# Transposed tokens copied by ScalarE, three experts' weights moved behind the first gathers, last attention pair normalised in two parts

## The chip, the cores and the metric

The kernel runs on one core of one Trainium2 chip. The metric is the device time of one execution in microseconds (us); lower is better. TensorE (PE) multiplies matrices, VectorE (DVE) and ScalarE (ACT) read its results from PSUM, GpSimd (POOL) issues most of the DMAs, SyncE (SP) issues the rest. Each engine works through its own instructions in order and waits on semaphores for the others.

## The reference

Two layers. The first is a block-causal attention over 8 batches, 8 heads, 576 positions and head size 64: scores in blocks of 64, softmax, times v. Its result, with heads side by side, is a matrix x of 4608 tokens by 512. The second is a mixture of experts with a given expert per token:

```python
x = attn_out.transpose(0, 2, 1, 3).reshape(B * S, H * D)      # 4608 x 512
for e in range(E):                                            # 8 experts
    mask = domain_id == e
    h = np.maximum(x[mask] @ w1[e], 0.0)                      # 512 -> 1024
    out[mask] = h @ w2[e]                                     # 1024 -> 512
```

## The kernel before

**Attention.** The 8 batches have 4 head pairs each, so there are 32 pairs p, and the loop at L469 emits pair p's scores (`emit_G`, L354) beside pair p-1's product with v (`emit_P` L408, `emit_Q` L413). For one pair PE transposes q and k of a later pair into PSUM tiles `PT` (L335), DVE copies them to `QK` (L339), PE makes scores into `ps` (L347, L373), ACT takes the exponential (L352), and PE multiplies by v into `po` (L398, L403), with a column of ones giving the row sums. At the end of `emit_Q` DVE takes a reciprocal (L419) and multiplies (L420) into the tile `x` of the batch, in half precision. `po` has two PSUM banks: blocks 1 to 3 of the pair in bank 0, blocks 4 and 0 in bank 1. `store_x` (L433) writes finished rows to the DRAM buffer `x_rows`, by SP; the last pair's 128 columns go out by one DMA of SP (64 rows) and one of ACT (512 rows).

**Weights.** `loads` (L450) runs on POOL's queue. From pair 20 on, it emits the weights of experts 0 to 3, two pieces per pair. An expert has 8 pieces (`w1_piece` L119, `w2_piece` L122), each read as 512 KB of single precision and written as 256 KB of half precision. 26 of the 32 pieces are emitted inside the pair loop; the other 6, of expert 3, at L609. POOL does not wait for the pairs there. A DMA on POOL's queue waits until the DMA issued eight places earlier has landed, since eight semaphores go round.

**Bridge.** After the last pair, PE runs 36 matmuls whose result is not used (L515). POOL gathers rows of `x_rows` by token index into `xg` (`gather`, L524; five indirect DMAs of 128 rows for an expert), and has to wait for every store of `x_rows`.

**Experts.** Each expert has 640 slots in five blocks of 128 tokens. `transpose_block` (L534) turns a gathered block on PE into a PSUM tile `pt` (L537, two buffers) and copies it to `xT` (L540, DVE). `mm1` (L553) makes eight groups of 8 matmuls (L559) into `ph` (two buffers), each followed by ACT's rectifier into `hT` (L565). `mm2` (L570) makes five blocks of 8 matmuls (L576) into `po` (two buffers); DVE copies each to `osb` (L582, ten buffers) and POOL scatters the rows to the output (L583). The transposes of expert e+1 stand between the blocks of `mm2` of expert e. For expert 0, `mm1` is run in two halves (L617): three blocks transposed, half 0, two more blocks, half 1. The gathers of expert e+2 stand ahead of `mm1` of expert e, and the weights of expert e+3 between the scatters of `mm2` of expert e, for e of 1 and more (L628).

A last loop (L636) handles experts with more than 640 tokens; its count is read from the data.

Of the kernel before, what the change touches and what calls it, by code (L numbers as in the profile page):

```python
# [9 lines left out]
F32 = mybir.dt.float32  # L10
# [3 lines left out]
ALU = mybir.AluOpType  # L14
# [4 lines left out]
def kernel(  # L19
# [10 lines left out]
    nc = tc.nc  # L30
    B, H, S, D = q.shape
    N = B * S
    E = moe_w1.shape[0]
    DM = moe_w1.shape[1]
# [2 lines left out]
    CAP = 128 * NB  # L37
    NJ = N // 128
    HP = H // 2
    NQ = NJ // 4  # L40

    ctx.enter_context(tc.manual_schedule())
    xd = nc.dram_tensor("x_rows", (N, DM), F16, kind="Internal").ap()
# [6 lines left out]
    asb = att.enter_context(tc.tile_pool(name="asb", bufs=1))  # L50
    aps = att.enter_context(
        tc.tile_pool(name="aps", bufs=1, space=bass.MemoryType.PSUM))
# [22 lines left out]
    def load_v(eng, b, ns):  # L75
# [11 lines left out]
        out=dom_i[:],  # L87
        in_=moe_domain_id.bitcast(I32).rearrange("(p c) -> p c", p=128))
    load_qk(0, 0, 1)
    for c in range(5):  # L90
        n = min(128, S - 128 * c)
        nc.sync.dma_start(
            out=vst[0][0:n, c],
            in_=v[0, :, 128 * c : 128 * c + n, :].rearrange("h p d -> p h d"))
# [4 lines left out]
    identh = const.tile([128, 128], F16, name="identh")  # L99
# [49 lines left out]
    def load_expert(e):  # L149
        if e % 4 == 3:  # L150
            w1s[e], w2s[e], t = load_vst(moe_w1[e], moe_w2[e])
        else:
            w1s[e], w2s[e], t = load_weights(wsb, 3, moe_w1[e], moe_w2[e])
        return t
# [12 lines left out]
    for i in range(2):  # L167
        n = 5 * HP * 66
        nc.scalar.copy(
            out=VE[i][:].rearrange("p m g z -> p (m g z)").bitcast(F32),  # L170
            in_=z_f[:].to_broadcast([128, n]))
        nc.scalar.copy(out=ATE[i][:, 64:832].bitcast(F32),
                       in_=z_f[:].to_broadcast([128, 384]))
# [4 lines left out]
    po = aps.tile([128, 2, 512], F32, name="po")  # L178
# [229 lines left out]
    def emit_P(st):  # L408
        for m in range(1, 4):
            emit_pv(st, m - 1, m)  # L410


    def emit_Q(st):  # L413
        hp = st["p"] % HP
        emit_pv(st, 3, 4)
        emit_pv(st, 4, 0)
        rc = asb.tile([128, 2, 3, 2], F32, name="rc", tag="rc", bufs=2)
        pv = po[:, :, 0:396].rearrange("p b (w z) -> p b w z", z=132)
        nc.vector.reciprocal(out=rc[:], in_=pv[:, :, :, 1:131:129])  # L419
        nc.vector.tensor_tensor(  # L420
            out=st["x"][:, :, 128 * hp : 128 * hp + 128].rearrange(
                "p (b w) (i z) -> p b w i z", b=2, i=2),
            in0=pv[:, :, :, 2:130].rearrange("p b w (i z) -> p b w i z", i=2),
            in1=rc[:].unsqueeze(4).to_broadcast([128, 2, 3, 2, 64]), op=ALU.mult)

    def emit_VE(b):
        for i in range(2):
# [2 lines left out]
                out=VE[b % 2][64 * i : 64 * i + 64, :, :, cs],  # L430
                in_=vS[b % 3][0:64, :, :, cs])

    def store_x(b, c0, c1, eng):  # L433
        x = xs[b]
        nc.sync.dma_start(out=xd[S * b : S * b + 64, c0:c1], in_=x[64:128, 4, c0:c1])
        eng.dma_start(
            out=xd[S * b + 64 : S * b + S, c0:c1].rearrange("(m p) d -> p m d", p=128),
            in_=x[:, 0:4, c0:c1])

    npair = B * HP  # L440
    rout, tabl = routing(), table()
    next(rout)
    QKs = {0: emit_T(0)}
# [3 lines left out]
    w1s, w2s, wts = {}, {}, []  # L447


    def loads(p):  # L450
        fn = nc.gpsimd.tensor_copy
        for b in range(2, B):
            if p == max(0, 4 * b - 10):
                load_qk(b)
                load_v(nc.gpsimd, b, range(0, 5))
                cast_v(fn, b - 1)
                load_v(nc.gpsimd, b, range(5, H + 1))
        if p == 4 * B - 12:
            cast_v(fn, B - 1)
            for e in range(4):  # L460
                wts.extend(load_expert(e))
        if p >= 4 * B - 12:
            for f in wts[:2]:
                f()
            del wts[:2]

    xs = []
    prev = None
    for p in range(npair + 1):  # L469
        b, hp = divmod(p, HP)  # L470
        st = None
        if p < npair:
            st = {"p": p, "QK": QKs.pop(p)}
            if hp == 0:
                x_t = asb.tile([128, 6, DM], F16, name="x", tag="x", bufs=4)
                xs.append(x_t)
            st["x"] = x_t
            emit_G(0, st)
        if p:
            if p + 2 < npair:  # L480
                QKs[p + 2] = emit_T(p + 2)
        if p < npair:
            emit_G(1, st)
        if prev is not None:
            emit_P(prev)
        if p < npair:
            emit_G(2, st)
        if prev is not None:
            emit_Q(prev)
            if prev["p"] == npair - 2:  # L490
                store_x(B - 1, 0, DM - 128, nc.sync)
            elif prev["p"] == npair - 1:
                store_x(B - 1, DM - 128, DM, nc.scalar)
            elif prev["p"] % HP == HP - 1:
                done = prev["p"] // HP
                for xb in {2: (0,), 3: (1,), 4: (2,), 5: (3, 4, 5), 6: (6,)}.get(done, ()):
                    store_x(xb, 0, DM, nc.sync)
        if p == 0:
            cast_v(nc.scalar.copy, 0)
            QKs[1] = emit_T(1)  # L500
            emit_VE(0)
            QKs[2] = emit_T(2)
        if p < npair and hp == 3 and b + 1 < B:
            emit_VE(b + 1)
        for _ in range(2 if p % 4 else 1):
            if p > 1:
                next(tabl, None)
        loads(p)
        prev = st
    for _ in tabl:  # L510
        pass

    ps = aps.tile([128, 2, 512], F32, name="ps", tag="ps", bufs=2)
    for i in range(36):
        nc.tensor.matmul(out=ps[:, i % 2], lhsT=identh[:], rhs=w1s[0][:, 0, 0:512],  # L515
                         start=True, stop=True)
    att.close()


# [1 line left out]
    mps = ctx.enter_context(  # L521
        tc.tile_pool(name="mps", bufs=1, space=bass.MemoryType.PSUM))

    def gather(tok):  # L524
        g = msb.tile([128, NB, DM], F16, name="xg", tag="xg", bufs=3)
        for blk in range(NB):
            nc.gpsimd.indirect_dma_start(  # L527
                out=g[:, blk, :], out_offset=None, in_=xd,
                in_offset=bass.IndirectOffsetOnAxis(
                    ap=tok[:, 1, blk : blk + 1], axis=0),  # L530
                bounds_check=N - 1, oob_is_err=False)
        return g

    def transpose_block(g, xT, blk):  # L534
        pt = mps.tile([128, 4, 128], F16, name="pt", tag="pt", bufs=2)
        for dc in range(4):
            nc.tensor.transpose(  # L537
                out=pt[:, dc], in_=g[:, blk, 128 * dc : 128 * dc + 128],
                identity=identh[:])
        nc.vector.tensor_copy(out=xT[:, :, 128 * blk : 128 * blk + 128], in_=pt[:])  # L540


    def w1_cols(w1h, dc, fc):
# [6 lines left out]
    def new_hT():  # L550
        return msb.tile([128, 8, CAP], F16, name="hT", tag="hT", bufs=2)

    def mm1(xT, hT, w1h, halves=(0, 1)):  # L553
        hw = CAP // 2
        for fc in range(8):
            ph = mps.tile([128, 2, 512], F32, name="ph", tag="ph", bufs=2)
            for dc in range(4):
                for i in halves:
                    nc.tensor.matmul(  # L559
                        out=ph[:, i, 0:hw],  # L560
                        lhsT=w1_cols(w1h, dc, fc),
                        rhs=xT[:, dc, hw * i : hw * i + hw],
                        start=(dc == 0), stop=(dc == 3))
            i0, i1 = halves[0], halves[-1] + 1
            nc.scalar.activation(  # L565
                out=hT[:, fc].rearrange("p (i n) -> p i n", i=2)[:, i0:i1],
                in_=ph[:, i0:i1, 0:hw], func=AF.Relu)
# [23 lines left out]
    def tok_of(e):  # L591
        return tok0[:, :, NB * e : NB * e + NB]
# [12 lines left out]
                                op0=ALU.arith_shift_right)  # L605
        nc.vector.memset(base_f[:], float(NB * E))

    xgs = {e: gather(tok_of(e)) for e in range(2)}
    for f in wts:  # L609
        f()  # L610
    xT = new_xT()
    for e in range(E):
        if e + 2 < E:
            xgs[e + 2] = gather(tok_of(e + 2))
        hT = new_hT()
        if e == 0:
            for i, blks in enumerate(((0, 1, 2), (3, 4))):  # L617
                for blk in blks:
                    transpose_block(xgs[0], xT, blk)
                mm1(xT, hT, w1s[0], (i,))  # L620
        else:
            mm1(xT, hT, w1s[e])
        nxt = None
        if e + 1 < E:
            xT = new_xT()
            nxt = (xgs[e + 1], xT)
        todo = ()
        if e and e + 3 < E:  # L628
            todo = load_expert(e + 3)
        if e == 1:  # L630
            count_rounds()
        mm2(hT, w2s[e], tok_of(e), outs[NB * e : NB * e + NB], todo, nxt)
# [50 lines left out]
```

## Time and profile before

The median of five runs is 335.2 us (333.94 to 336.11). The profiled execution took 334.62 us, of which the profile's span covers 333.0 us.

| what | value |
|---|---|
| profiled execution, whole | 334.62 us |
| its span | 333.0 us |
| PE busy | 273.8 us, 82% of the span |
| DVE busy | 160.3 us, 48% |
| ACT busy | 146.1 us, 44% |
| POOL busy | 205.4 us, 62% |
| mean granted clock of PE | 0.945 |
| last product with v, start | 145.39 us |
| first gather, start | 152.19 us |
| first matmul of `mm1`, expert 0 | 158.84 us |
| first matmul of `mm2`, expert 0 | 172.42 us |
| last matmul block ends about | 319.5 us |

Times are from the start of the span. In the tables a line names its source line (L559), the engine, the operation, output and inputs by the names in the program, and the idle time of the engine just before it with what ended that idle time. PEld is PE's loading of stationary operands, which runs beside its matmuls. The end of a matmul in the trace is a model, its start is measured. The granted clock is the share of full speed at which PE was allowed to run.

### The profile page before, as it was taken

To read this page: it belongs to the slowest core of one execution; us is meant where nothing else is said; L and a number is where in the kernel's file an instruction comes from. 1 tells how busy PE (TensorE), PEld (TensorE's weight loads), DVE (VectorE), ACT (ScalarE), POOL (GpSimd) and SP (SyncE) were. 2 spreads that over 40 slices of the span, in tenths; PEclk is the share of its full clock that TensorE was granted. 3 is DMA by queue.
4 is the path that set the end of the run, shared out by engine and by line. 5 is a ranking of instruction groups with operands and counts; after the bars stand their busy time and mean duration, and the time that the engine had idled before them with its cause. 6 is when DMAs were issued, how large, how long until landed. Compare 5 with 4: busy or idle time off the path is not lost. (4 is left out here: it accounts for less than half of the span.)

```text
span 333.0 us, 8592 instructions
## 1 busy us (share of the span) xinstructions
PE 273.8 (82%) x3658; PEld 176.9 (53%) x3658; DVE 160.3 (48%) x298; ACT 146.1 (44%) x208; POOL 205.4 (62%) x274
## 2 busy tenths in 40 slices
PE   2588787947899987885899789989898998999930
PEld 1366555635577765552555455647465564656510
DVE  3869899979789787621015123050422404042120
ACT  5658556827499877820350331505033150513200
POOL 8669999899883643205884718767785875223230
PEclk9999789959699999999699999999999999999995
DMA  8999999999991999992395309959798894112030
GB/s 162 201 214 209 176 260 193 243 207 189 240 267 28 205 212 231 216 245 64 106 178 184 113 18 194 263 118 237 189 214 213 153 237 150 74 46 96 32 114 0
DMA packets 36472, 55.68 MB, mean 167 GB/s; under 512 B 9838, under 2 KB 22638, under 8 KB 36432
## 3 DMA queue, kind: packets, MB, share of 16 engines
q0 software_dynamic: 26128, 49.17, 68.3%
q1 hardware_dynamic: 9776, 5.81, 6.5%
q8 instruction: 30, 0.49, 0.6%
q10 hardware_dynamic: 528, 0.13, 0.2%
q14 instruction: 10, 0.08, 0.1%
HBM read 67.15 MB, written 15.20 MB: 247 GB/s over the span
## 5 line engine op out<-in xcount | busy, mean ns | idle before, releaser
L352 ACT ACTIVATE A<-ps 128x1024 f16<-128x1024 f32 (+1 forms) x96 | 83.1, 883 | 42.3 <-PE ps L347 30.1
L565 ACT ACTIVATE hT<-ph 128x640 f16<-128x640 f32 (+1 forms) x72 | 46.1, 644 | 121.6 <-PE ph L559 97.8
L583 POOL DMA_INDIRECT out_dram<-osb,tok x40 | 40.5, 1012 | 55.4 <-DVE osb L582 43.5
L540 DVE COPY xT<-pt 128x512 f16<-128x512 f16 x40 | 16.9, 424 | 111.2 <-PE pt L537 85.7
L559 PE MATMUL ph<-xT,w1h 128*128 128x320 f16 x384 | 56.8, 307 | 5.2 <-issue 2.5
L576 PE MATMUL po<-w2h,hT 128*128 128x512 f16 x240 | 56.7, 379 | 3.2 <-DVE osb L582 2.7
L527 POOL DMA_INDIRECT xg<-x_rows,tok x40 | 40.5, 1012 | 26.1 <-DMA x_rows<-x 14.2
L559 PEld LDWEIGHTS <-w1h 128*128 128x128 f16 x384 | 38.4, 100 | 23.4 <-issue 6.2
L78 POOL DMA_DIRECT2D vst<-in_v_dram x56 | 42.5, 786 | 10.1 <-DMA kh<-in_k_dram 4.3
L576 PEld LDWEIGHTS <-hT 128*128 128x128 f16 x320 | 30.1, 98 | 34.4 <-issue 4.9
L339 DVE COPY QK<-PT 128x576 f16<-128x576 f16 x64 | 45.6, 749 | 3.2 <-PE PT L335 2.9
L347 PE MATMUL ps<-QK 64*128 64x512 f16 (+3 forms) x256 | 37.0, 328 | 2.7 <-ACT A L352 1.1
L403 PE MATMUL po<-vS,A 128*128 128x65 f16 x640 | 36.5, 201 | 1.3 <-issue 1.3
L398 PE MATMUL po<-VE,ATE 128*128 128x130 f16 x160 | 32.9, 232 | 4.6 <-DVE x L420 3.5
L582 DVE COPY osb<-po 128x512 f32<-128x512 f32 x40 | 27.4, 684 | 18.8 <-PE po L576 18.8
L403 PEld LDWEIGHTS <-A 128*128 128x128 f16 x640 | 32.0, 102 | 4.0 <-issue 4.0
L420 DVE TENSOR_TENSOR x<-po,rc 128x768 f16<-128x768 f32 x32 | 30.6, 957 | 1.1
L335 PE MATMUL PT<-identh,kh 64*64 64x64 f16 x576 | 17.0, 204 | 10.8 <-DVE inv L234 6.0
L114 POOL CAST vS<-vst 128x1024 f16<-128x1024 f32 (+1 forms) x21 | 19.1, 962 | 5.9 <-DVE QK L339 5.9
L335 PEld LDWEIGHTS <-kh 64*64 64x64 f16 x576 | 14.8, 119 | 12.3 <-issue 9.6
L398 PEld LDWEIGHTS <-ATE 128*128 128x128 f16 x160 | 16.0, 100 | 9.5 <-issue 7.3
L335 PE MATMUL PT<-identh,qh 64*64 64x64 f16 x576 | 16.7, 203 | 4.1 <-DVE QK L339 3.4
(88 smaller groups left out, 274.9 us busy)
## 6 DMA issues: line engine op xcount, KB each, us to landing
vst<-in_v_dram POOLq DMA_DIRECT2D x63, 128.0 KB
w1h<-in_moe_w_dram POOLq DMA_DIRECT2D x24, 256.0 KB
w2h<-in_moe_w_dram POOLq DMA_DIRECT2D x24, 256.0 KB
vst<-in_moe_w_dram POOLq DMA_DIRECT2D x16, 256.0 KB
qh<-in_q_dram POOLq DMA_DIRECT2D x14, 288.0 KB
kh<-in_k_dram POOLq DMA_DIRECT2D x14, 288.0 KB
x_rows<-x SPq DMA_DIRECT2D x7, 512.0 KB, 11.1
vst<-in_v_dram SPq DMA_DIRECT2D x4, 256.0 KB, 5.9
```

The costliest lines, as they stand in the source:

```text
L78: eng.dma_start(out=vst[b % 3][:, 0:4, n], in_=v[b, n, 0:512, :].rearrange("(c p) d -> p c d", p=128))
L335: nc.tensor.transpose(out=PT[h, j], in_=src[h, hp, 64 * j : 64 * j + 64], identity=identh[h, h])
L339: nc.vector.tensor_copy(out=QK[:, s].rearrange("p (n j) -> p n j", j=9), in_=PT[:].rearrange("p j n -> p n j"))
L347: nc.tensor.matmul(out=o[:, i], lhsT=QK[h, 1, 128 * c : 128 * c + 128], rhs=QK[h, 0, 64 + 128 * c : S], start=True, stop=True)
L352: nc.scalar.activation(out=o, in_=i, func=AF.Exp, scale=0.125)
L398: nc.tensor.matmul(out=o[:, 1:131], lhsT=st["AE"][:, 128 * m : 128 * m + 128], rhs=VE[b % 2][:, m, hp, 1:131], start=True, stop=(m == 0))
L403: nc.tensor.matmul(out=o[:, 1 + 65 * i : 66 + 65 * i], lhsT=at_block(st, i, c, m), rhs=vS[b % 3][:, c, hp, 1 + 65 * i : 66 + 65 * i], star ...
L527: nc.gpsimd.indirect_dma_start(out=g[:, blk, :], out_offset=None, in_=xd, in_offset=bass.IndirectOffsetOnAxis(ap=tok[:, 1, blk : blk + 1], ...
L559: nc.tensor.matmul(out=ph[:, i, 0:hw], lhsT=w1_cols(w1h, dc, fc), rhs=xT[:, dc, hw * i : hw * i + hw], start=(dc == 0), stop=(dc == 3))
L565: nc.scalar.activation(out=hT[:, fc].rearrange("p (i n) -> p i n", i=2)[:, i0:i1], in_=ph[:, i0:i1, 0:hw], func=AF.Relu)
L576: nc.tensor.matmul(out=po[:], lhsT=hT[:, fc, 128 * blk : 128 * blk + 128], rhs=w2h[:, fc, :], start=(fc == 0), stop=(fc == 7))
L583: nc.gpsimd.indirect_dma_start(out=dst[blk], out_offset=bass.IndirectOffsetOnAxis(ap=tok[:, 0, blk : blk + 1], axis=0), in_=osb[:], in_off ...
```

## The change

Seven edits, of which the fourth has two places:

1. `transpose_block` copies `pt` to `xT` by ACT in place of DVE, for all experts.
2. Inside the pair loop only expert 0's 8 pieces are emitted, one per pair from 20 to 27.
3. Behind the pair loop POOL's queue reads: gather of expert 0; four w1 pieces of expert 1; gather of expert 1; four w2 pieces of expert 1; gather of expert 2; eight pieces of expert 2. Expert 3's eight pieces stand between the scatters of expert 0's `mm2`.
4. The last pair is normalised in two parts: bank 0 behind `emit_P` (`emit_norm(prev, 0, 1)`), bank 1 at the end of `emit_Q`. Its rows are stored by three DMAs: three blocks by SP early, then one block by ACT and 64 rows by SP.
5. The 36 unused matmuls write to a `PT` buffer in place of `ps`.
6. Behind the transposes of blocks 0 and 1 of expert 0, five more unused matmuls each.
7. `npair` is set earlier in the file.

```diff
     def emit_Q(st):
-        hp = st["p"] % HP
         emit_pv(st, 3, 4)
         emit_pv(st, 4, 0)
-        rc = asb.tile([128, 2, 3, 2], F32, name="rc", tag="rc", bufs=2)
-        pv = po[:, :, 0:396].rearrange("p b (w z) -> p b w z", z=132)
+        if st["p"] < npair - 1:
+            emit_norm(st, 0, 2)
+        else:
+            emit_norm(st, 1, 2)
+
+    def emit_norm(st, b0, b1):
+        hp = st["p"] % HP
+        nb = b1 - b0
+        rc = asb.tile([128, nb, 3, 2], F32, name=f"rc{nb}", tag=f"rc{nb}", bufs=2)
+        pv = po[:, b0:b1, 0:396].rearrange("p b (w z) -> p b w z", z=132)
         nc.vector.reciprocal(out=rc[:], in_=pv[:, :, :, 1:131:129])
...
+    def store_w(b, w0, w1, c0, c1, eng):
+        eng.dma_start(
+            out=xd[S * b + 64 + 128 * w0 : S * b + 64 + 128 * w1, c0:c1].rearrange(
+                "(m p) d -> p m d", p=128),
+            in_=xs[b][:, w0:w1, c0:c1])
...
         if p == 4 * B - 12:
             cast_v(fn, B - 1)
             for e in range(4):
-                wts.extend(load_expert(e))
-        if p >= 4 * B - 12:
-            for f in wts[:2]:
-                f()
-            del wts[:2]
+                wts.append(load_expert(e))
+        if 4 * B - 12 <= p < 4 * B - 4:
+            wts[0][p - 4 * B + 12]()
...
         if prev is not None:
             emit_P(prev)
+            if prev["p"] == npair - 1:
+                emit_norm(prev, 0, 1)
+                store_w(B - 1, 0, 3, DM - 128, DM, nc.sync)
...
             elif prev["p"] == npair - 1:
-                store_x(B - 1, DM - 128, DM, nc.scalar)
+                store_w(B - 1, 3, 4, DM - 128, DM, nc.scalar)
+                nc.sync.dma_start(
+                    out=xd[S * (B - 1) : S * (B - 1) + 64, DM - 128 : DM],
+                    in_=xs[B - 1][64:128, 4, DM - 128 : DM])
...
-    ps = aps.tile([128, 2, 512], F32, name="ps", tag="ps", bufs=2)
-    for i in range(36):
-        nc.tensor.matmul(out=ps[:, i % 2], lhsT=identh[:], rhs=w1s[0][:, 0, 0:512],
-                         start=True, stop=True)
+    def warm(t, n):
+        for i in range(n):
+            nc.tensor.matmul(out=t[:], lhsT=identh[:], rhs=w1s[0][:, 0, 0:512],
+                             start=True, stop=True)
+
+    warm(aps.tile([128, 512], F32, name="PT", tag="PT", bufs=2), 36)
...
-        nc.vector.tensor_copy(out=xT[:, :, 128 * blk : 128 * blk + 128], in_=pt[:])
+        nc.scalar.copy(out=xT[:, :, 128 * blk : 128 * blk + 128], in_=pt[:])
...
-    xgs = {e: gather(tok_of(e)) for e in range(2)}
-    for f in wts:
+    xgs = {0: gather(tok_of(0))}
+    for f in wts[1][:4]:
+        f()
+    xgs[1] = gather(tok_of(1))
+    for f in wts[1][4:]:
         f()
     xT = new_xT()
     for e in range(E):
         if e + 2 < E:
             xgs[e + 2] = gather(tok_of(e + 2))
+        if e == 0:
+            for f in wts[2]:
+                f()
...
                 for blk in blks:
                     transpose_block(xgs[0], xT, blk)
+                    if blk < 2:
+                        warm(mps.tile([128, 512], F32, name="po", tag="po", bufs=2), 5)
...
-        todo = ()
+        todo = wts[3] if e == 0 else ()
```

More of the change, by code (lines that the diff above doesn't have):

```diff
@@ L39 @@
     HP = H // 2
+    npair = B * HP
     NQ = NJ // 4
@@ L413, in emit_Q @@
     def emit_Q(st):
-        hp = st["p"] % HP
         emit_pv(st, 3, 4)
         emit_pv(st, 4, 0)
-        rc = asb.tile([128, 2, 3, 2], F32, name="rc", tag="rc", bufs=2)
-        pv = po[:, :, 0:396].rearrange("p b (w z) -> p b w z", z=132)
+        if st["p"] < npair - 1:
[7 more added lines that the diff above has]
+        pv = po[:, b0:b1, 0:396].rearrange("p b (w z) -> p b w z", z=132)
         nc.vector.reciprocal(out=rc[:], in_=pv[:, :, :, 1:131:129])
         nc.vector.tensor_tensor(
-            out=st["x"][:, :, 128 * hp : 128 * hp + 128].rearrange(
-                "p (b w) (i z) -> p b w i z", b=2, i=2),
+            out=st["x"][:, 3 * b0 : 3 * b1, 128 * hp : 128 * hp + 128].rearrange(
+                "p (b w) (i z) -> p b w i z", b=nb, i=2),
             in0=pv[:, :, :, 2:130].rearrange("p b w (i z) -> p b w i z", i=2),
-            in1=rc[:].unsqueeze(4).to_broadcast([128, 2, 3, 2, 64]), op=ALU.mult)
+            in1=rc[:].unsqueeze(4).to_broadcast([128, nb, 3, 2, 64]), op=ALU.mult)
     def emit_VE(b):
@@ L438, in store_x @@
             in_=x[:, 0:4, c0:c1])
-    npair = B * HP
     rout, tabl = routing(), table()
```

## The prediction

> **What bounds the kernel now.** I read the page first (busy shares, slices), then the instructions in order of time around the places where PE stops, then stretches with clock and DMA share. PE is busy 82% of the span, so the question is where it waits. The first view is the page's slices of 8.3 us each: granted clock of PE in tenths, and busy share of the DMA engines.
>
> ```profile
> PEclk9999789959699999999699999999999999999995
> DMA  8999999999991999992395309959798894112030
> ```
>
> The clock falls once after the attention, in the slice at 158 us. DMA is saturated from 114 to 150 us, then nearly idle until 166: the weights come while attention still runs. Stretches say the same with numbers (busy time of each engine, clock, DMA share, GB/s):
>
> ```profile
> 113.00:137.00 24.00, 20.31 (x528) 14.91 (x525) 18.47 (x31) 18.59 (x27) 9.19 (x17) 1.00 1.12 216
> 144.00:150.00 6.00, 5.45 (x47) 2.97 (x48) 1.69 (x3) 0.00 (x0) 0.00 (x0) 1.00 1.07 245
> 157.00:163.00 6.00, 4.77 (x20) 2.76 (x21) 0.81 (x2) 1.31 (x3) 4.48 (x6) 0.50 0.30 94
> ```
>
> In the saturated stretch PE stops where it waits for nothing that the trace shows. PE in order of time:
>
> ```profile
> 118.81 0.38 PE L335 MATMUL PT<-identh,kh 64*64 64x64 f16 x13
> 120.36 0.25 PE L335 MATMUL PT<-identh,kh 64*64 64x64 f16 x5 [1.17 <-issue]
> ...
> 131.20 0.22 PE L398 MATMUL po<-VE,ATE 128*128 128x130 f16 x1
> 132.75 0.28 PE L403 MATMUL po<-vS,A 128*128 128x65 f16 x4 [1.33 <-issue]
> ```
>
> A third such stop is at 125.3 us. Counting PE's records, the three are exactly 256 instructions apart, and 256 is the size of one packet of PE's instruction queue (page: 30 packets, 0.49 MB). The packets before the stops start at 117.96, 124.17 and 130.48 us, about 1 us ahead of each stop, though with DMA unsaturated (96.95, 100.86, 104.88 us) none causes a stop. So the weights hold up PE's instructions.
>
> Then the bridge: the last stores leave at 146.90 and the first gather starts 5.3 us later.
>
> ```profile
> 146.90 0.45 SPq L435 DMA_DIRECT2D x_rows<-x  x1
> 146.90 0.41 ACTq L436 DMA_DIRECT2D x_rows<-x  x1
> 152.19 1.10 POOL L527 DMA_INDIRECT xg<-x_rows,tok  x1 [14.16 <-DMA x_rows<-x]
> ```
>
> Last, the experts. An undisturbed expert takes 18.4 us (8.9 for `mm1`, 9.5 for `mm2`; expert 6). `mm1` of expert 1 takes 13.0 (182.1 to 195.15), and `mm2` of experts 2 to 5 take 10.56, 10.78, 10.74 and 11.13: together 9.3 us lost (4.1 and 5.1). ACT's rectifiers in the first of these:
>
> ```profile
> 186.23 0.70 ACT L565 ACTIVATE hT<-ph 128x640 f16<-128x640 f32 x1 [1.06 <-PE ph L559]
> 189.12 0.70 ACT L565 ACTIVATE hT<-ph 128x640 f16<-128x640 f32 x1 [2.18 <-PE ph L559]
> 192.00 1.30 ACT L565 ACTIVATE hT<-ph 128x640 f16<-128x640 f32 x2 [2.18 <-PE ph L559]
> ```
>
> ACT, free, starts up to 2.5 us after the matmuls it waits for were issued, where 0.25 is usual: PE's signal comes late. In `mm2` of expert 2 (DVE, PE and POOL):
>
> ```profile
> 215.32 0.39 PE L537 MATMUL pt<-identh,xg 128*128 128x128 f16 x4
> 215.38 1.00 POOL L527 DMA_INDIRECT xg<-x_rows,tok  x1 [0.31 <-issue]
> 217.45 0.42 DVE L540 COPY xT<-pt 128x512 f16<-128x512 f16 x1 [3.22 <-remote]
> 217.79 0.68 DVE L582 COPY osb<-po 128x512 f32<-128x512 f32 x1
> 218.53 1.89 PE L576 MATMUL po<-w2h,hT 128*128 128x512 f16 x8 [0.88 <-DVE osb L582]
> ```
>
> The transposes are issued at 215.32, their signal is recorded at 217.43, the copy starts at 217.45, `osb` stands behind it on DVE, and PE waits 0.88 for `osb` to free a `po` buffer. All of these losses fall beside gathers.
>
> **The change part by part.** *Weights out of the attention.* Expert 0's pieces will still leave at once: POOL issued pieces from 107.8 on, 0.53 apart, without regard to pairs. They fill DMA until about 118 (2.1 MB at 216 GB/s is 9.7 us). The other 18 pieces that ran here are gone. Starts of the normalisation (L420) give the pair time: 3.00 undisturbed, 3.48 with the copies of `VE`, but 3.94, 4.21 and 4.49 in the pairs that hold the stops; 0.94 + 1.21 + 1.01 = 3.2 us. The packet of the first stop was already late while only expert 0's weights were in flight, so I take 2.5; bounds 0 (the stops remain) and 3.2. The Trainium skill, "Runtime: NRT & Kernel Launch", section "Instruction fetch mechanics", calls the cost of crossing such a 16 KB boundary mostly hidden, which would make this term 0; the stops of 1.2 us here disagree, and I go by them.
>
> *Bridge.* Let A be the start of the 36 unused matmuls, 145.4 before. Before: gather A+6.8, first transposes A+9.9, `mm1` A+13.4, its end A+26.7. Splitting the last normalisation into two adds a reciprocal (0.23) and starts some 0.3 earlier, so the last stores leave at A+1.4 to A+1.5 as now; on SP the early store (0.59 of issue) is done before the last. But DMA is idle then: landing takes 1.9 (shortest x store in the trace) in place of 4.3, and the 384 KB store of A-0.4 lands by A+3.5 (0.6 issue, 1.6 at 245 GB/s, 1.9). One more us lies between landing and gather (151.2 to 152.19): gather A+4.5. Data to transposes takes 3.1: A+7.6, but the 36 matmuls (7.9) hold PE to A+8.0. Transposes 0.39, five unused matmuls 1.08 (36 in 7.93), twice: block 2 ends at A+11.4. ACT's copy costs 0.60 by its exponential of 128x512, where DVE's was 0.42; with 0.25 for the signal, `mm1` starts at A+12.2. Half 0 ran at clock 0.50 and took 7.1; half 1, at full clock, 4.65. PE has no gap over 1 us now, so I take 4.65: A+16.9. Half 1 waits for two ACT copies queued behind the last rectifier: 0.2 + 0.44 + 2 x 0.60, so A+18.7 (the gap is 1.85 against 1.5), and ends at A+23.4. That is 3.3 less; late signals beside gathers cost about 0.6, as now: 2.7. Bounds 0 (clock stays low, 2.4 lost, and the unused matmuls delay by 0.9) and 3.3.
>
> *Copies on ACT.* 35 copies go to ACT inside `mm2`, 5 x 0.60 = 3.0 us of 9.5 in which ACT has no rectifiers; hidden by the matmuls, as the last of the five is ready 1.1 us before the next `mm1`. No new function table is loaded: the trace has one load at the start, for copies, exponentials and rectifiers alike. The gain: `osb` no longer stands behind a copy whose signal is late. But the signal is PE's, and the first `osb` has a signal of its own that can be late too. The losses in `mm2` have bounds 0 and 5.1. The 4.1 in `mm1` of expert 1 isn't touched by the copies; but gathers move. By POOL's rows (gather of five 6.6, four pieces 2.2, scatters with pieces 11.2 to 11.9) the gather of expert 3 begins at A+45, with `mm2` of expert 1 from A+42 on, and later ones fall into `mm2` too. In `mm2` a signal may be 1 us late before PE stops (1.95 - 0.68 - 0.25), in `mm1` 0.15 (1.09 - 0.70 - 0.25). Bounds for all: 0 and 9.3; a loss would need more gathers, and there are 40 as before. I take half, 5, since neither end is nearer. The Trainium skill, "SBUF — State Buffer", section "Who interferes with whom", says that DVE's fast copies and a GpSimd operation lock each other out of a shared port; then all 5.1 in `mm2` would go. Against it, a copy at 201.20 runs its 0.43 in full beside a scatter that started at 201.11, and ACT's waits were late as well.
>
> *Weights behind the gathers.* POOL adds 18 pieces, 9.9 us, after A. Scatters of expert 0 stand behind expert 2's pieces and start at A+33 where A+26.9 (3.5 after `mm2`, as at 175.88) is the earliest; ten `osb` buffers cover that. The gather of expert 3 lands its first block at A+48, needed at A+60. Costed at 0; cover 12 us. The edits in names and in the `PT` target cost nothing on PE: same matmul, same count.
>
> Sum: 334.6 - 2.5 - 2.7 - 5.0 = 324.4. The median of the runs is 0.6 above the profiled time; I say 324.5.
>
> **The rivals.** *Late signals stay* (ACT waits as DVE did): 334.6 - 2.5 - 2.7 = 329.4. For it: ACT's own rows at 186 to 192. Against: the in-order chain copy, `osb`, PE is cut. *All losses go:* 334.6 - 3.2 - 3.3 - 9.3 = 318.8. *Weights come too late (slower):* 24 pieces of three experts stand ahead of the gather of expert 3. Pieces paced by landing went 1.43 apart (113.25 to 137.50). At that pace it lands 24 x 0.88 = 21 us later, 9 us too late: 329.4 + 9 = 338. It decides from a spacing of 1.06. Against it: from 199 us on, pieces between scatters went at 0.55. *No net effect:* stops, clock and signals only change place.
>
> **How the numbers follow.** Forecast (321 to 327) 0.43, late signals (327 to 332) 0.29, all gone (317 to 320.5) 0.12, weights late 0.12, no net effect 0.04. About 0.5% is what a measurement here tells from no change. Faster 0.84, same 0.04, slower 0.12. The range 317.5 to 332 leaves out the last two cases and edges.
>
> **What would show it.** Right: no PE stop of 1.2 us between 119 and 133; first gather 4.5 after the unused matmuls start; clock 1.0 through `mm1` of expert 0; `mm2` of experts 2 to 5 near 9.5. Wrong: PE waiting for gathered rows or for weights in experts 1 to 3, or rectifiers and ACT copies starting 2 us behind their matmuls.

## The result and the profile after

The changed kernel takes 332.87 us (median of 42 runs, 327.18 to 339.22), the kernel before 334.54 (median of 79, 330.12 to 339.89). The ratio is 0.9902, with a 95% interval of 0.9878 to 0.9927: 3.3 us faster (2.4 to 4.1), where 10 were forecast. The medians differ by 1.7 us only: they hold all executions, while the ratio leaves out those more than 1.5% above the fastest of their kernel. The profiled execution took 332.68 us, its span is 331.0.

The page's slices of the changed kernel, clock in tenths and DMA share, show that the first part of the change is there. DMA is no longer full at the end of the attention (its digits are 1 or 2 from the 16th slice, at 124 us, to 157 us), and there is no low clock where expert 0 begins (9 from the 19th slice, at 149 us, to the 27th; the 7 in the 28th is a stretch at clock 0.50 from 224.8 to 228.2 us, in `mm1` of expert 3). The 8 in the 18th slice, 141 to 149 us, is a stretch of 3.4 us at clock 0.50 that begins at 146.3 us.

```profile
PEclk9999797887699999989999999997999999999985
DMA  8999899989993791222998997999989795212030
```

Stretches of the changed kernel (busy time of each engine, clock, DMA share, GB/s):

```profile
113.00:137.00 24.00, 22.30 (x579) 16.33 (x579) 19.81 (x35) 20.67 (x30) 0.71 (x2) 1.00 0.58 122
144.00:150.00 6.00, 5.12 (x37) 2.43 (x37) 1.51 (x4) 0.00 (x0) 0.00 (x0) 0.72 0.35 101
```

From 113 to 137 us PE is busy 22.3 us in place of 20.3 and DMA share falls from 1.12 to 0.58. Two of the three stops of PE are gone. One is left, while expert 0's pieces still fill DMA: its share is 1.05 to 1.14 from 112 to 124 us and 0.42 in the next 2 us. The forecast had them done at about 118.

```profile
120.41 0.38 PE L336 MATMUL PT<-identh,kh 64*64 64x64 f16 x13
121.96 0.25 PE L336 MATMUL PT<-identh,kh 64*64 64x64 f16 x5 [1.17 <-issue]
```

The bridge, in order of time. The first gather starts 3.8 us after the last stores, where it was 5.3; they land in 2.7 us in place of 4.3:

```profile
146.88 0.45 SPq L509 DMA_DIRECT2D x_rows<-x  x1
146.88 0.37 ACTq L443 DMA_DIRECT2D x_rows<-x  x1
150.71 1.11 POOL L547 DMA_INDIRECT xg<-x_rows,tok  x1 [37.00 <-issue]
```

Ahead of it stands a wait that is new. PE is free at 144.6 and goes on at 145.51, when DVE has normalised bank 0:

```profile
144.90 0.56 DVE L428 TENSOR_TENSOR x<-po,rc 128x384 f16<-128x384 f32 x1
145.51 0.22 PE L399 MATMUL po<-VE,ATE 128*128 128x130 f16 x1 [0.88 <-DVE x L428]
```

And the late signals have not gone. Set against an undisturbed expert (first to last matmul 8.9 us for `mm1`, 9.7 for `mm2`), the kernel before loses 4.1 us in `mm1` of expert 1 and 5.1 in `mm2` of experts 2 to 5; the changed one loses 7.2 in `mm1` of experts 2, 3 and 4 and 2.1 in `mm2` of experts 4 and 5. Both sums are 9.2. ACT and PE in `mm1` of expert 3, where rectifiers are late:

```profile
220.97 0.70 ACT L585 ACTIVATE hT<-ph 128x640 f16<-128x640 f32 x1 [3.04 <-PE ph L579]
...
223.78 1.30 ACT L585 ACTIVATE hT<-ph 128x640 f16<-128x640 f32 x2 [2.12 <-PE ph L579]
224.54 2.87 PE L579 MATMUL ph<-xT,vst 128*128 128x320 f16 x11 [1.57 <-ACT hT L585]
```

At the start of `mm1` of expert 4 it is ACT's copy of transposed tokens that waits for PE's signal, and then PE waits for the copy:

```profile
242.15 0.59 ACT L560 COPY xT<-pt 128x512 f16<-128x512 f16 x1 [3.65 <-PE po L596]
242.79 2.47 PE L579 MATMUL ph<-xT,w1h 128*128 128x320 f16 x17 [1.10 <-ACT xT L560]
```

So ACT as the copying engine gets late signals as DVE did.

Where the two profiled executions differ, by the starts of instructions in both traces:

| stretch | before | after | difference |
|---|---|---|---|
| start to the normalisation in pair 20 (nothing changed there) | 108.9 | 110.5 | +1.6 |
| eight pairs from there | 28.4 | 26.2 | -2.2 |
| from there to the 36 unused matmuls (A) | 8.2 | 9.2 | +1.0 |
| A to the end of `mm1` of expert 0 | 26.8 | 24.5 | -2.3 |
| to `mm1` of expert 1 | 9.9 | 9.8 | -0.1 |
| `mm1` of expert 1 to the last matmul | 137.0 | 137.0 | 0.0 |
| to the end of the span | 13.9 | 13.8 | -0.1 |

But for rounding the sum is the difference of the spans, -2.0 us. So of the 4.5 us that the eight pairs and the stretch from A on give, 1.0 is given back ahead of A, and the experts give nothing.

### The profile page after: what moved, and what is told of

It reads as the page before. It is cut to its first block, busy times and chain, and to the rows that moved or that the text cites. A ratio compares the mean times of both kernels' runs of the same rounds, so it can differ in the third digit from the quotient of the medians.

```text
span 331.0 us, 8633 instructions
## 1 busy us (share of the span) xinstructions
PE 278.4 (84%) x3668; PEld 179.4 (54%) x3668; DVE 147.0 (44%) x260; ACT 168.5 (51%) x248; POOL 206.6 (62%) x274
## 5 line engine op out<-in xcount | busy, mean ns | idle before, releaser
L579 PE MATMUL ph<-xT,w1h 128*128 128x320 f16 x384 | 54.5, 299 | 4.4 <-ACT xT L560 1.8
L560 ACT COPY xT<-pt 128x512 f16<-128x512 f16 x40 | 23.1, 586 | 55.9 <-PE pt L557 32.7
L579 PEld LDWEIGHTS <-w1h 128*128 128x128 f16 x384 | 37.5, 98 | 21.2 <-issue 6.2
L348 PE MATMUL ps<-QK 64*128 64x512 f16 (+3 forms) x256 | 37.9, 336 | 2.7 <-ACT A L353 1.1
L428 DVE TENSOR_TENSOR x<-po,rc 128x768 f16<-128x768 f32 (+1 forms) x33 | 30.8, 933 | 1.1
L579 PE MATMUL ph<-xT,vst 128*128 128x320 f16 x128 | 19.7, 316 | 2.1 <-ACT hT L585 1.6
```

The source lines that it names most:

```text
L348: nc.tensor.matmul(out=o[:, i], lhsT=QK[h, 1, 128 * c : 128 * c + 128], rhs=QK[h, 0, 64 + 128 * c : S], start=True, stop=True)
L579: nc.tensor.matmul(out=ph[:, i, 0:hw], lhsT=w1_cols(w1h, dc, fc), rhs=xT[:, dc, hw * i : hw * i + hw], start=(dc == 0), stop=(dc == 3))
```

## The experiments

Each group of four ran on one chip, with runs of the kernel before on the same chip beside them. On these three chips the kernel before takes 323.6, 324.3 and 324.0 us, 10 us less than in the first comparison.

**The last pair in one part again.** Edit 4 undone in the changed kernel.

```diff
-        if st["p"] < npair - 1:
-            emit_norm(st, 0, 2)
-        else:
-            emit_norm(st, 1, 2)
+        emit_norm(st, 0, 2)
...
-            if prev["p"] == npair - 1:
-                emit_norm(prev, 0, 1)
-                store_w(B - 1, 0, 3, DM - 128, DM, nc.sync)
...
-                store_w(B - 1, 3, 4, DM - 128, DM, nc.scalar)
-                nc.sync.dma_start(
-                    out=xd[S * (B - 1) : S * (B - 1) + 64, DM - 128 : DM],
-                    in_=xs[B - 1][64:128, 4, DM - 128 : DM])
+                store_x(B - 1, DM - 128, DM, nc.scalar)
```

> The changed kernel with its last pair normalised in one part again (edit 4 undone). Theory A (the two parts make PE wait): in the changed kernel the product of the last two blocks starts 0.88 us after PE is free, since it waits for the normalisation of bank 0. Undone, that wait goes, the 36 unused matmuls start about 1.0 us sooner after the last but one normalisation, and the bridge's low clock (146 to 150 us) is less likely; the kernel is 1 us faster than the changed one, about 330.5 against before at 334.5. Rival B (the split is worth its smaller last stores): the last DMAs land later, the first gather starts 0.3 to 0.5 us later against the start of the unused matmuls, and the time stays or grows by 0.5 us.

Measured: 318.56 us against 323.64, ratio 0.9834 (0.9795 to 0.9872). PE in order of time at the end of the attention of this kernel:

```profile
146.50 0.34 PE L404 MATMUL po<-vS,A 128*128 128x65 f16 x6
146.68 0.22 PE L399 MATMUL po<-VE,ATE 128*128 128x130 f16 x1
...
147.03 1.67 PE L524 MATMUL PT<-w1h,identh 128*128 128x512 f16 x7
148.49 0.45 SPq L447 DMA_DIRECT2D x_rows<-x  x1
```

The products of bank 1 follow those of bank 0 without a gap. From the normalisation of pair 27 to A it takes 11.14 us, as in before (11.16); three kernels below that keep the two parts take 12.18 (the one with the copies on VectorE, the changed kernel unaltered, and the one without the ten unused matmuls), and the one with plain DMAs 12.44. (Two more kernels below with one part take 11.8 and 11.9; in these, and in the one with plain DMAs, the clock falls to 0.50 between 1.2 and 1.7 us ahead of A.) So the two parts cost 1.04 us (12.18 less 11.14): theory A for the wait. In return the gather starts 4.8 to 5.1 us after A with two parts and 5.3 with one, so up to 0.5 comes back, as rival B had it; but A itself is a whole microsecond later. The net 0.5 us or more is below what the time of this kernel can tell, so the gain of 1 us that theory A expected in the time is not shown.

**The copies on VectorE again.** Edit 1 undone in the changed kernel.

```diff
-        nc.scalar.copy(out=xT[:, :, 128 * blk : 128 * blk + 128], in_=pt[:])
+        nc.vector.tensor_copy(out=xT[:, :, 128 * blk : 128 * blk + 128], in_=pt[:])
```

> The changed kernel with the transposed tokens copied by VectorE again (edit 1 undone). Theory A (the late completions are PE's, and who copies doesn't matter): the sum lost in the experts against 8.7 us for mm1 and 9.6 for mm2 stays near 9 us, as in the changed kernel and in before, and the time is within 1 us of the changed kernel. Rival B (the copies' place matters): mm2 loses about 1 us for each expert beside a gather, 4 to 5 us more than the changed kernel.

Measured: 319.44 us, ratio 0.9834 (0.9776 to 0.9892). Neither expectation held as written: nothing is lost in the experts at all. Every expert takes the undisturbed 18.4 us. DVE in `mm2` of expert 2, behind a gather that POOL issued from 209 to 215.5 us and beside scatters from 215.8 us on:

```profile
218.82 0.42 DVE L560 COPY xT<-pt 128x512 f16<-128x512 f16 x1 [8.23 <-PE pt L557]
220.77 0.42 DVE L560 COPY xT<-pt 128x512 f16<-128x512 f16 x1 [1.53 <-PE pt L557]
221.12 0.68 DVE L602 COPY osb<-po 128x512 f32<-128x512 f32 x1
222.72 0.42 DVE L560 COPY xT<-pt 128x512 f16<-128x512 f16 x1 [0.93 <-PE pt L557]
```

The copies keep their 0.42 us and start on time. On this chip, where no signal was late, the place of the copies is worth nothing; whether it is worth something where signals are late can't be read from it.

**The order of the weights alone.** Edits 2 and 3 in the kernel before. Run twice, on two chips.

```diff
             for e in range(4):
-                wts.extend(load_expert(e))
-        if p >= 4 * B - 12:
-            for f in wts[:2]:
-                f()
-            del wts[:2]
+                wts.append(load_expert(e))
+        if 4 * B - 12 <= p < 4 * B - 4:
+            wts[0][p - 4 * B + 12]()
...
-    xgs = {e: gather(tok_of(e)) for e in range(2)}
-    for f in wts:
+    xgs = {0: gather(tok_of(0))}
+    for f in wts[1][:4]:
+        f()
+    xgs[1] = gather(tok_of(1))
+    for f in wts[1][4:]:
         f()
```

> The kernel before with the order of the weights alone changed (edits 2 and 3). Theory A: two of the three PE stops of 1.2 us in pairs 23 to 27 go and the first gather starts about 1 us sooner after the last store; 3 us faster than before. Rival B (DMA that leaves attention comes back in the experts): gathers or weights are late there, and the time is that of before, or 3 us more.

> The kernel before with the order of the weights alone changed (edits 2 and 3), once more for its interval. Theory A (the weights' order is the whole gain): ratio 0.982 to 0.988 to before, equal to the whole change or better by up to 0.5%. Rival B (the early gather needs the other edits to pay): 0.99 or more.

Measured: 320.68 us against 323.64 (0.9871, 0.9783 to 0.9958), and 320.06 against 324.04 (0.9789, 0.9719 to 0.9858). Theory A: within these intervals this order alone gives what the whole change gives. A stretch of the second run, to be set against the first of the stretches in the prediction:

```profile
113.00:137.00 24.00, 21.98 (x554) 16.08 (x552) 19.12 (x32) 21.73 (x32) 0.00 (x0) 1.00 0.48 112
```

There is no PE stop in pairs 23 to 27 of either run. The gather starts 4.7 and 5.1 us after A, and `mm1` of expert 0 ends 22.1 and 23.7 us after A, against 23.4 in the changed kernel at full clock (below). The difference between 22.1 and 23.7 is a stretch of 3.4 us at clock 0.50 inside `mm1` in the second.

Over all traces, the two of the first comparison included, the stretch from A to the end of `mm1` of expert 0 takes 26.8 to 31.1 us in the four with the old order of weights and 22.1 to 24.5 in the ten with the new order. The eight pairs from pair 20 on take 27.5 to 29.0 in the old order. In the new they take 25.2 to 28.4 where the clock stays full, and 27.6 to 30.2 in four kernels where it falls to 0.50 for 3.4 or 6.8 us. By these traces the bridge carries most of the gain on the later chips, and the gain in the attention can't be told from the length of one trace.

**Plain DMAs in place of the gathers**, in the changed kernel; the choice of rows by token is left out.

```diff
-            nc.gpsimd.indirect_dma_start(
-                out=g[:, blk, :], out_offset=None, in_=xd,
-                in_offset=bass.IndirectOffsetOnAxis(
-                    ap=tok[:, 1, blk : blk + 1], axis=0),
-                bounds_check=N - 1, oob_is_err=False)
+            nc.gpsimd.dma_start(
+                out=g[:, blk, :], in_=xd[N - CAP + 128 * blk : N - CAP + 128 * blk + 128, :])
```

> The changed kernel with every gather replaced by a plain DMA on POOL's queue of the last 640 rows of x_rows: the choice of rows by token is left out, so all experts compute on the same rows. Bytes, waits and order stay. Theory A (gathers by index delay PE's completions): rectifiers and copies start 0.25 us after their matmuls throughout, the 9.5 us lost in mm1 and mm2 of experts 2 to 5 go, and the time falls by 8 to 10 us to about 323. Rival B (something else of the same period, such as PE's instruction packets or the weights): the losses stay, and the time falls by less than 2 us.

Measured: 319.47 us, ratio 0.9856 (0.979 to 0.9922). Inconclusive: on this chip there were no late completions to take away, with gathers or without.

**The changed kernel on another chip**, unaltered.

> The changed kernel again, beside the kernel before on the same chip. Theory A (the late completions belong to a chip, not to either kernel): where the kernel before shows none, mm1 and mm2 of experts 1 to 7 take 8.7 and 9.7 us here, and the ratio to before is 0.984 to 0.987, about 4.5 us, all of it from pair 20 to mm2 of expert 0; where before shows them, so does this kernel, and the ratio is 0.99. Rival B (the change moves the late completions but can be rid of them): the experts take less than those of before by 5 us or more.

Measured: 320.69 us against 324.3, ratio 0.9857 (0.9797 to 0.9916). From `mm1` of expert 1 to the last matmul it takes 127.8 us, where it took 137.0 in the first trace. Theory A in so far as the loss of 9.2 us is not the kernel's. This is also the trace to hold the bridge's working against, since the clock is full through it (PE and ACT in order of time):

```profile
156.38 0.38 PE L557 MATMUL pt<-identh,xg 128*128 128x128 f16 x4 [0.56 <-PE PT L533]
156.92 0.58 ACT L560 COPY xT<-pt 128x512 f16<-128x512 f16 x1 [11.65 <-DMA xg<-x_rows,tok]
...
159.40 0.58 ACT L560 COPY xT<-pt 128x512 f16<-128x512 f16 x1 [0.72 <-PE pt L557]
160.04 4.94 PE L579 MATMUL ph<-xT,w1h 128*128 128x320 f16 x32 [0.67 <-ACT xT L560]
```

A is 147.9 here: gather at A+4.8, `mm1` at A+12.2, its end at A+23.4.

**Without the ten unused matmuls** between expert 0's transposes. Edit 6 undone in the changed kernel.

```diff
-                    if blk < 2:
-                        warm(mps.tile([128, 512], F32, name="po", tag="po", bufs=2), 5)
```

> The changed kernel without the ten unused matmuls between the transposes of expert 0 (edit 6 undone). Theory A (they only hold PE, since the gather is early enough by now that PE never idles for 3 us): mm1 of expert 0 starts 0.9 to 1.1 us sooner after the 36 unused matmuls start, its half 0 stays at full clock (4.8 us), and the kernel is 1 us faster than the changed one. Rival B (they keep the clock up): half 0 takes 6 to 7 us, and the kernel is 1 to 2 us slower.

Measured: 321.9 us, ratio 0.9806 (0.9752 to 0.9859), not told apart from the changed kernel. The trace has both effects: `mm1` starts at A+11.6 in place of A+12.2, and then runs into a low clock, so that it ends at A+24.3 in place of A+23.4.

```profile
155.00:159.00 4.00, 4.00 (x19) 2.37 (x18) 0.00 (x0) 1.41 (x4) 3.39 (x6) 0.57 0.84 158
```

Over all traces with the new order of weights: of the five with the ten unused matmuls none has a low clock inside `mm1` of expert 0; of the five without them three have (this one, the second with the weights' order alone, and the one with 30 unused matmuls). They cost 0.6 us and save about 1.5 when they save; if that is in three of five, it comes out about even, and ten traces are few to say so.

**The copies on ScalarE alone**, in the kernel before (the line of edit 1). Run twice.

> The kernel before with the copies of the transposed tokens on ScalarE, and nothing else changed (edit 1 alone). Theory A (the copies are hidden either way): the time of before within 1 us, with half 1 of expert 0 waiting 0.4 us more for its copies. Rival B (VectorE was the bound in mm2): 4 to 5 us faster, all of it in mm2 of experts 2 to 5.

> The kernel before with edit 1 alone, once more, since its 1.1% loss was of few runs at a low clock. Theory A (the copies are hidden either way, but half 1 of expert 0 waits 0.4 us more): within 0.5% of before. Rival B (the copies on ScalarE cost 3 us by themselves): 1% slower again, with the loss in a place that the trace shows against z1_before.

Measured: 326.51 us against 324.3 (1.0108, 1.0056 to 1.0159), then 325.1 against 324.04 (1.0010, 0.9974 to 1.0045). The loss of the first did not come back in the second, which had twice the runs; its mean granted clock was 0.938, and 0.945 in the second. Theory A, with the first left as a miss. There is no gain in either, but the traces of both show no late signal (127.8 us from `mm1` of expert 1 to the last matmul), so there was no loss that the copies could have taken away.

**The order of the weights with 30 unused matmuls in place of 36.**

```diff
-    for i in range(36):
+    for i in range(30):
```

> The kernel before with the order of the weights changed (edits 2 and 3) and 30 unused matmuls in place of 36; copies on VectorE, last pair in one part, none between the transposes. Theory A (the weights' order is the whole gain, and the other edits cost 1 to 2 us): 5 to 6 us faster than before and 1 to 2 us faster than the changed kernel. Rival B (with fewer unused matmuls the clock falls before mm1 of expert 0): half 0 takes 6 to 7 us and the gain is 3 us or less.

Measured: 319.52 us, ratio 0.9873 (0.9829 to 0.9918). In its trace PE waits for the gather at full clock and meets a low clock in `mm1`, as rival B had it: half 0 takes 6.2 us. Its gain of 4.1 us (2.7 to 5.5) is more than the 3 us of rival B, and the time can't be told from that of the other kernels with this order.

**The kernel before, for its trace.**

> The kernel before again, to have its trace from a chip of these runs. Theory A (the late completions belong to the chip of the first two traces): where the other kernels here take 127.8 us from mm1 of expert 1 to the last matmul, this one does too, although its transposed tokens are copied by VectorE and its gathers start where they started; from the 36 unused matmuls to mm1 of expert 1 it takes about 36.5 us, 3 to 4 more than with the weights moved. Rival B (the old order of gathers and copies makes them late): it takes about 137 us there again, and the changed order is what got rid of them.

Measured: ratio 1.0007 (0.9965 to 1.0049). This settles that the loss in the experts does not belong to the old program. The stretch from `mm1` of expert 1 to the last matmul, first in the first trace of before, then in the first trace of the changed kernel, then in this one, last in the changed kernel unaltered on another chip (length, then busy PE, PEld, DVE, ACT, POOL, clock, DMA share, GB/s):

```profile
182.10:319.10 137.00, 129.21 (x848) 78.03 (x847) 35.78 (x75) 39.26 (x56) 78.64 (x93) 1.00 0.60 146
```

```profile
180.15:317.19 137.04, 130.45 (x849) 78.58 (x847) 25.88 (x45) 55.94 (x86) 86.68 (x104) 0.99 0.74 178
```

```profile
180.50:308.20 127.70, 127.70 (x848) 77.83 (x847) 36.09 (x75) 39.37 (x56) 78.59 (x93) 1.00 0.64 157
```

```profile
181.00:308.90 127.90, 127.90 (x849) 77.79 (x847) 25.60 (x45) 56.30 (x86) 86.68 (x105) 1.00 0.82 193
```

The kernel before, with the same copies on DVE and the same gathers, loses 9.2 us there in one trace and nothing in the other, and so does the changed kernel. Whether the chip or another condition makes the difference is not shown. ACT in `mm1` of expert 1 of this trace, where 2.18 us of waiting stood before:

```profile
182.85 0.70 ACT L565 ACTIVATE hT<-ph 128x640 f16<-128x640 f32 x1 [0.38 <-PE ph L559]
183.94 0.70 ACT L565 ACTIVATE hT<-ph 128x640 f16<-128x640 f32 x1 [0.38 <-PE ph L559]
```

The trace also shows what the weights can do to the bridge in the old order. The last stores leave at 141.05 while weights fill DMA (its share is 1.12 from 137 to 144 us and 0.98 from 144 to 150) and land 9.4 to 9.6 us later. The gather starts 12.0 us after A, where it was 6.8 in the first trace, and `mm1` of expert 1 starts 40.9 us after A, where about 36.5 was expected:

```profile
141.05 0.45 SPq L435 DMA_DIRECT2D x_rows<-x  x1
141.06 0.41 ACTq L436 DMA_DIRECT2D x_rows<-x  x1
151.58 1.10 POOL L527 DMA_INDIRECT xg<-x_rows,tok  x1 [13.46 <-DMA x_rows<-x]
```

**Expert 0's weights ahead of the last cast of v**, on top of the new order.

```diff
-            cast_v(fn, B - 1)
             for e in range(4):
                 wts.append(load_expert(e))
-        if 4 * B - 12 <= p < 4 * B - 4:
-            wts[0][p - 4 * B + 12]()
+            for f in wts[0]:
+                f()
+            cast_v(fn, B - 1)
```

> The kernel with the order of the weights changed (edits 2 and 3) and expert 0's eight pieces ahead of the last cast of v on POOL's queue, so that they run from about 100 us, where DMA is idle, in place of 107. Theory A (DMA full of weights holds up PE's instruction packets): the stop of 1.2 us in pair 23 goes too, and the kernel is 1 us faster than with edits 2 and 3 alone. Rival B (the stop is a matter of that place in the program, or the pieces now meet the loads of q, k and v): it stays or moves to another pair, and the time is the same.

Measured: 319.31 us, ratio 0.9841 (0.9784 to 0.9897), the same as with the new order alone. The stop in pair 23 is gone, but stops of 1.1, 1.8 and 1.3 us begin at 101.2, 107.3 and 113.9 us: rival B. Each is at a multiple of 256 instructions from the others (matmuls and weight loads counted together), and DMA is full of weights, q, k and v there. So the stops go with PE's count of instructions and with a full DMA, not with a pair; that it is the packets of instructions that come late is the reading that fits this.

## Why the prediction was wrong

**Attention, -2.5: right for the first traces.** Eight pairs lost 2.2 us there, which is the second and third stop (1.21 and 1.01). The four kernels with the old order have three, two, one and two such stops in pairs 23 to 27, the ten with the new order have one or none, all while expert 0's pieces land; in the last experiment the stops moved with the weights. The Trainium skill, "Runtime: NRT & Kernel Launch", section "Instruction fetch mechanics", which the prediction set against the stops, calls such a crossing mostly hidden. Over the fourteen traces, from 40 to 150 us, PE stopped for over 0.9 us at none of the 75 crossings at which DMA's share in the 2 us before was under 0.9, and at 27 of the 159 others. So "mostly" holds, but a full DMA is where it fails.

**Bridge, -2.7: the sum held, in part by luck, and a wait was left out.** With the clock full, the points come out nearly as written: gather A+4.8 (4.5), `mm1` A+12.2 (12.2), end A+23.4 (23.4). Some errors cancel. The last stores leave at A+1.0 and not A+1.4, but land in 2.7 us and not 1.9; the transposes start at A+8.5 and not A+8.0, but follow each other in 1.30 us and not 1.47. Two things were not in the sum. First, "splitting the last normalisation into two adds a reciprocal and starts some 0.3 earlier" looked at DVE alone. What was late next was PE: its products for bank 1 wait for DVE's reading of bank 0, 1.0 us. They write another bank; that they wait because both banks are one tile in the program is likely but was not tried. Second, in the first trace the clock fell at 146.3 us for 3.4 us, and the 36 unused matmuls took 9.5 us in place of 7.9 and held PE back. "Clock stays low" had been a bound for `mm1`, not for the matmuls ahead of it.

**Experts, -5.0: this is the step that failed.** It was half of 9.3 us, taken "since neither end is nearer". The measured value is 0.0: 137.0 us in both first traces, and 127.8 in all twelve kernels of the experiments, before and after alike. The right reading was in the same paragraph (the signal is PE's, and ACT waits for it as DVE does), and the first rival, 329.4, was built on it; the row of ACT's copy at 242.15 shows it.

The other half of the argument, that gathers move into `mm2`, where a signal may be 1 us late, had the place of the gathers wrong. The gather of expert 3 was forecast at A+45. It starts at A+50.6, 7.4 us into `mm2` of expert 1: the scatters of expert 0 with expert 3's pieces between them were taken to last 11.2 to 11.9 us from A+33, and they last 14.9 from A+34.3.

```profile
196.44 1.08 POOL L547 DMA_INDIRECT xg<-x_rows,tok  x1 [1.30 <-DMA vst<-in_moe_w_dram]
```

That `mm2` loses nothing, and the `mm1` behind it, where 0.15 us is all the room there is, loses 1.8 us; the next gather begins at 215.0 us in `mm2` of expert 2 and it is `mm1` of expert 3 that loses 4.1 (a part of it at the low clock of 224.8 us). Whether ACT's copies took the 3 us off `mm2` and the later gathers put them on `mm1`, or the late signals only fell elsewhere, was not told apart, as edit 1 alone was run only where no signal was late.

The statement on the shared port (the Trainium skill, "SBUF — State Buffer", section "Who interferes with whom") would have given all of the 5.1 us in `mm2`. The page has it for copies in a two-port mode, and no run here shows that these copies, which read PSUM, are in one. Against it stand the late signals that remain with no copy of tokens on DVE, and the copies on DVE that ran their 0.42 us beside POOL's DMAs. The ratio of 1.0010 with the copies on ScalarE alone says nothing about it, since nothing was late there.

**Weights behind the gathers, 0: right.** From 161.2 us on PE is busy without a gap in the second run of the order alone, at a DMA share of 0.83; the rival of late weights (338) did not occur.

The nearest rival is that of the late signals: -5.2 for attention and bridge. Taking off the 1.0 us of the two parts leaves -4.2, and the runs have -3.3 (2.4 to 4.1) in the first comparison and, for the eight kernels with the new order of weights and real gathers on three chips, ratios of 0.979 to 0.987, some 4 to 7 us (2.4 to 5.1 by their medians). That the later chips give more is no success of the -5.0, as their experts had nothing to gain.

## What to carry to other kernels

A loss that the trace puts beside the work one changes is not thereby a loss of that work: when a consumer that did nothing else waits for a completion signal just as long as the busy one, moving the copy has no reason to shorten it, and the term is zero until a run shows otherwise. When a step is cut in two to start sooner, ask who else waits for the tile that its first half reads, not only when the half itself can start. And transfers that are hidden by compute still cost if they fill DMA, because stores that gate the next stage come later (here they landed in 9.4 us with DMA full and in 2.7 without), and PE stopped for 1 to 2 us at some multiples of 256 of its instructions.

## What the runs showed of the hardware

- PE's completions came up to some 2.5 us late beside or just after gathers, whichever engine waited for them (ACT's rectifiers, DVE's copies before, ACT's copies after), in both kernels, in the first two traces only (9.2 us for the experts), and in none of the twelve kernels run later on three chips. The times agree with it: before takes 334.5 us in the first comparison, 324 in the others. What makes them late, the chip or another condition, was not found; plain DMAs in place of gathers could only be tried where they did not occur.
- PE stopped for 0.9 to 2.5 us at 27 of 159 multiples of 256 of its instructions (matmuls and weight loads) with DMA's share at 0.9 or more in the 2 us before, and at none of 75 with a lower share (fourteen traces, 40 to 150 us). Why most crossings pass without a stop under a full DMA is open.
- The granted clock falls to 0.50 for 3.4, 6.8 or 10.2 us at a time (longer behind the last matmul), at places that change from trace to trace of much the same program: the time to pair 20, which no edit touches, was 102.3 to 111.2 us. That is more than the whole effect of the change, and a single profile can't tell a gain of 3 us in this kernel.
